# Sparse attention and a feed-forward layer on one core: the local heads in blocks of 32 queries, turned by VectorE and small transfers

## The chip, the core and the metric

The kernel runs on one core of a Trainium2 chip. The core has TensorE (PE, matrix products), VectorE (DVE), ScalarE (ACT), GpSimd (POOL) and SyncE (SP, which here issues all transfers). The metric is the device time of one execution in microseconds (us). Three runs of the kernel before took 927.29, 929.12 and 929.34 us, a median of 929.12.

## The reference

Attention over 8 batches, 8 heads, 576 tokens and 64 channels a head, followed by a feed-forward layer over the 4608 tokens. Four heads see the last 32 tokens ("local"), four see every 32nd token ("strided").

```python
scores = scale * np.matmul(q, k.transpose(0, 1, 3, 2))
rel = pos[:, None] - pos[None, :]
mask_local = (rel >= 0) & (rel < stride)                       # stride = 32
mask_strided = (rel >= 0) & (pos[None, :] % stride == pos[:, None] % stride)
masks = [mask_local if h < H // 2 else mask_strided for h in range(H)]
attn = softmax(np.where(masks, scores, -1e9))
x = np.matmul(attn, v)                                         # to (4608, 512)
h = x @ w_in                                                   # (512, 2048)
return (0.5 * h * (1.0 + erf(h / sqrt(2)))) @ w_out            # (2048, 512)
```

## The kernel before

**The feed-forward layer** sets the frame. The tokens are cut into 12 tiles of 384. For each tile 16 steps run, one for each block of 128 hidden channels, so there are 192 steps, numbered n = 0 to 191. In a step `ffn_h(n)` (L537 to L539) multiplies the tile's x by a block of w_in into a bank H of PSUM: twelve products of 384 columns, since x and w are each split into a high and a low part. `ffn_g(n)` takes the GELU on ACT (L546), rounds it on ACT (gh, L548), and forms the rest gl on DVE (L550). `ffn_o(n)` (L576 to L578) adds nine products of 512 columns to three banks O. H has two banks, so step n + 2 can begin its H only when gl of step n has read the bank. `ffn_o(n)` is issued two steps after `ffn_h(n)`.

**The strided heads** are done by DVE alone: a long row of small products and sums (L412, L454), which are given out over the steps by their estimated cost, in advance of the tile that needs them.

**The local heads** are cut into 36 jobs of 128 tokens (two windows of 64 queries, each with 96 keys, four heads); three jobs fill one tile. `local_job(x)` makes, in this order: scores of 64 queries against 96 keys on PE, into the four column blocks of one bank (L247); masking with a running minimum on DVE (L204); the exponential on ACT (L209); the sum's reciprocal on DVE (L213, L216); the scaling by it on ACT (L225); four transpositions on PE (L253); the copy of their result out of PSUM on ACT (L255); the products with v on PE (L262); and the split of the result into the high and low part of x, xh on ACT (L229) and xl on DVE (L231). Jobs 0 to 5 belong to the opening, whose order is written out by hand in a table. The 30 jobs from 6 on belong to the main loop, which begins at step 16: `stage(n)` moves every job under way on by two parts a step, and `starts` says at which step a job begins, every fifth step as a rule. So PE meets a job in three places: scores, transpositions three steps later, and products with v one step after these.

**What sets the order.** In the main loop only ACT follows the order in which the code is written. A scheduler places the instructions of PE, DVE, POOL and SP, by its own estimate of when their inputs are ready; every engine then executes its own list in order, and waits where an input is missing. SP's list holds the loads of q and k (`qk`), of v (`vl`), of the strided heads' data (`sq`, `sk`, `sv`), and the stores of the result (`ob`). POOL builds the masks and clears the strided scores (`sc`, L405).

Of the kernel before, what the change touches and what calls it, by code (L numbers as in the profile page):

```python
# [10 lines left out]
F32 = mybir.dt.float32  # L11
# [20 lines left out]
NEG = -8.0e9  # L32
# [13 lines left out]
NB = 16  # L46
# [33 lines left out]
LPLACE = [(b, r // 2) for _, b, r in ROWS[::2]]  # L80
# [3 lines left out]
def attn_ffn_kernel(ctx: ExitStack, tc: tile.TileContext, qk, vl, qka, va, qs, ks, vs, w, out):  # L84
    nc = tc.nc
    NJ = qk.shape[0]
    NR, D = qs.shape[2:]
    S = NR * STRIDE
    HL = P // STRIDE
    NT, DM = out.shape  # L90
    NF = w.shape[0]
    NC = DM // P
    NU = len(PLACE)
    NV = len(VISITS)
    NTILE = NT // TT
# [12 lines left out]
    lpool = ctx.enter_context(tc.tile_pool(name="lpool", bufs=2))  # L108
# [3 lines left out]
    ps_a = ctx.enter_context(tc.tile_pool(name="ps_a", bufs=1, space=bass.MemoryType.PSUM))  # L112
# [2 lines left out]
    smask = const.tile([P, MA], F32, name="smask")  # L115
    mask = const.tile([P, LK], F32, name="mask")
    mask0 = const.tile([P, LK], F32, name="mask0")

    def rows(j):
        return slice(j * D, (j + 1) * D)  # L120
# [4 lines left out]
    def slot(name, shape, dtype=F32):  # L125

        return wpool.tile(shape, dtype, name=name, tag="w")
# [41 lines left out]
    def x_tile(t):  # L169
        if t not in xt:  # L170
            xt[t] = [xpool.tile([P, NC, TT], F32R, name=f"x{i}_{t}", tag=f"x{i}{t % 2}") for i in "hl"]
        return xt[t]


    jq, jv = {}, {}
    loaded = set()

    def load_jq(x):
        if x < NJ and ("q", x) not in loaded:
            loaded.add(("q", x))  # L180
            jq[x] = lpool.tile([P, 2 * N2 * (LU + LK)], F32, name=f"qk_{x}", tag="qk", bufs=3)
            nc.sync.dma_start(jq[x], qk[x])

    def load_jv(x):
        if x < NJ and ("v", x) not in loaded:
            loaded.add(("v", x))
            jv[x] = lpool.tile([LK, 2, HL, D], F32, name=f"vl_{x}", tag="vl", bufs=4)
            nc.sync.dma_start(jv[x], vl[x])

    def buffers(name, pn):  # L190
        n = 4 * LK
        if pn >= 0:
            return pbig[pn][:, 0:n], pbig[pn][:, n:n + DM]
        return (lpool.tile([P, n], F32, name=f"P_{name}", tag="P", bufs=2),
                lpool.tile([P, DM], F32, name=f"PT_{name}", tag="PT", bufs=2))

    def small(name):
        return [lpool.tile([P, 4], F32, name=f"{k}_{name}", tag=k, bufs=4) for k in ("nm", "ss", "rs")]
# [29 lines left out]
    def to_x(dh_, dl_, src):  # L228
        nc.scalar.copy(dh_, src)  # L229
        yield  # L230
        nc.vector.tensor_tensor(dl_, src, dh_.bitcast(F32), ALU.subtract)  # L231

    def local_job(x, banks=None, dve=0, pn=-1):

        s, pt = [pl.tile([P, DM], F32, name=f"S{i}_L{x}", tag=tg)
                 for i, (pl, tg) in enumerate(banks or ((ps_a, "S0"), (ps_a, "S1")))]
        p, pts = buffers(f"L{x}", pn)
        nb = 2 * N2
        blocks = [slice(i * LK, (i + 1) * LK) for i in range(nb)]
        qv = jq[x][:, 0:nb * LU].rearrange("p (i t) -> p i t", t=LU)  # L240
        kv = jq.pop(x)[:, nb * LU:].rearrange("p (i t) -> p i t", t=LK)
        msk = [mask0 if LPLACE[2 * x + i % 2][1] == 0 else mask for i in range(nb)]
        steps = softmax_parts(blocks, P, lambda i: s[:, blocks[i]], lambda i: msk[i], p,
                              *small(f"L{x}"), dve)
        for i, cs in enumerate(blocks):
            for j in (i % 2, 1 - i % 2):
                nc.tensor.matmul(s[rows(j), cs], qv[rows(j), i, :], kv[rows(j), i, :], start=True, stop=True)  # L247
        for st in steps:
            yield
            st()  # L250
        yield
        for i, cs in enumerate(blocks):
            nc.tensor.transpose(pt[:LK, i * P:(i + 1) * P], p[:, cs], ident)  # L253
        yield
        nc.scalar.copy(pts[:LK, 0:nb * P], pt[:LK, 0:nb * P])  # L255
        yield
        xp = s if banks else ps_a.tile([P, DM], F32, name=f"X_L{x}", tag="X")
        xv = xp[:, 0:N2 * P].rearrange("p (a q) -> p a q", a=N2)
        for i in range(nb):
            pr, a = divmod(i, 2)  # L260
            for j in range(2):
                nc.tensor.matmul(xv[rows(j), pr, a * LU:(a + 1) * LU], jv[x][:, a, 2 * pr + j, :],  # L262
                                 pts[:LK, i * P + j * LU:i * P + (j + 1) * LU], start=True, stop=True)
        jv.pop(x)
        if x >= JPT:
            load_jv(x + 3)
        yield
        t, c0 = divmod(x * P, TT)
        dst = [a[:, 0:N2, c0:c0 + P] for a in x_tile(t)]
        yield from to_x(*dst, xv)  # L270


# [91 lines left out]
    for vi in range(NA, NV):  # L364
        n = VISITS[vi][2]
# [163 lines left out]
    ready = [t * NF for t in range(NTILE)]  # L529
    xfree = [0, 0] + ready[1:-1]  # L530

    def ffn_h(n):
        t, f = divmod(n, NF)
        xh, xl = xt[t]
        hp = ps_h.tile([P, TT], F32, name=f"H_{n}", tag="H")
        for c in range(NC):
            nc.tensor.matmul(hp, w1[f][:, 0, c, :], xh[:, c, :], start=(c == 0), stop=False)  # L537
            nc.tensor.matmul(hp, w1[f][:, 0, c, :], xl[:, c, :], start=False, stop=False)  # L538
            nc.tensor.matmul(hp, w1[f][:, 1, c, :], xh[:, c, :], start=False, stop=(c == NC - 1))  # L539
        hps[n] = hp  # L540
# [78 lines left out]
    for j in range(2):  # L619
        nc.gpsimd.affine_select(mask[rows(j)], mask[rows(j)], pattern=[[-1, LK]], compare_op=ALU.is_ge,  # L620
                                fill=NEG, base=STRIDE, channel_multiplier=1)
        nc.gpsimd.affine_select(mask[rows(j)], mask[rows(j)], pattern=[[1, LK]], compare_op=ALU.is_ge,
                                fill=NEG, base=-1, channel_multiplier=-1)
    nc.gpsimd.tensor_copy(mask0[:, STRIDE:], mask[:, STRIDE:])
    nc.gpsimd.memset(mask0[:, 0:STRIDE], NEG)
    for h in range(HL):
        m = smask[h * 32:(h + 1) * 32]
        nc.gpsimd.iota(m.bitcast(I32), pattern=[[-1, MA]], base=0, channel_multiplier=1)
# [54 lines left out]
    for nm in "qkv":  # L683
        load_strided(order_g[1], nm)

    active = []

    def start_local(x, **kw):
        active.append([local_job(x, **kw), x, 0])
        advance(active[-1])  # L690
        load_jq(x + 3)

    def advance(e, k=2):
        for _ in range(k):
            if next(e[0], True) is not None:
                active.remove(e)
                break
        e[2] += 1

    def stage(n):  # L700
        if any(e[2] == 1 for e in active):
            flush_exps(NU)
        for e in list(active):
            if e[2] < 4 or n >= xfree[e[1] // JPT]:
                advance(e)

    starts = {}
    for i in range(JPT):
        for t in range(2, NTILE):
            starts[max(NB, ready[t - 1] + 5 * i - 2)] = t * JPT + i  # L710

    def step(n):
        c = n // NF
        while splits and n >= xfree[splits[0][0]]:
            for _ in splits.pop(0)[1]():
                pass
        if c > 0:
            stage(n)
        if n in starts:
            start_local(starts[n])  # L720
        if c + 1 < NTILE:
            a, e = ready[c] + (1 if c == 0 else 0), ready[c + 1]
            need = last[c] + (last[c + 1] - last[c]) * min(1.0, max(0.0, (n - a + 1) / (e - a - 2)))
            run_strided(max(need, tot * (n - N0) / (ready[-1] - 2 - N0)))
        if NB <= n < NS:
            ffn_h(n)
            for _ in ffn_g(n):
                pass
        if n == NS + 1:
            ffn_o(n - 3, n - 2)  # L730
        elif n >= NB + 2 and n < NS:
            ffn_o(n - 2)
        if n >= NB + 2 and (n - 2) % NF == NF - 1:
            store((n - 2) // NF)

    with tc.manual_schedule(engines={ET.Activation}):
        for n in range(NB, NS + 1):
            step(n)
    with tc.manual_schedule(engines={ET.Activation, ET.PE}):
# [66 lines left out]
```

## Time and profile before

| | |
|---|---|
| runs | 927.29, 929.12, 929.34 us |
| profiled execution, whole | 928.01 us |
| its span from first to last instruction | 926.2 us |
| mean granted clock of TensorE | 0.987 |
| DMA, mean | 67 GB/s, share of the 16 engines 20% |

The span covers the opening up to about 115 us, in which weights are loaded and split and x for the first tiles is made; then the main loop to about 922 us; then one last copy and store. In the timelines each row gives the start in us, the length in us, the engine, the line of the code, the operation, what it writes and reads with shapes, and in brackets the idle time before it with what ended it. Matrix products overlap in their lengths, so their pace is read from one start to the next. PEld is the load of a product's stationary operand. On DVE too, short instructions overlap and are read from start to start.

### The profile page before, as it was taken

The numbers are of one execution on the slowest core, as the hardware profiler recorded it, in microseconds if no ns is written. First come the engines' busy times: TensorE is split into PE (matmuls) and PEld (weight loads), VectorE is DVE, ScalarE is ACT, GpSimd is POOL, SyncE is SP. The second block draws the span as 40 slices with busy tenths as digits, with TensorE's granted clock in tenths as the row PEclk, the third lists the DMA queues.
The fourth block names the chain that finished last, engine by engine and source line by source line (L and its number), as shares of the span: only waits on it lengthen the run. The fifth ranks groups of instructions, "written<-read, shape, count | busy, mean of one in ns | idle before, by whom it ended". The sixth has DMA issues, their size and how long they took to land.

```text
span 926.2 us, 17928 instructions
## 1 busy us (share of the span) xinstructions
PE 897.7 (97%) x5588; PEld 791.2 (85%) x5588; DVE 703.7 (76%) x4834; ACT 490.6 (53%) x1115; POOL 8.0 (1%) x56
## 2 busy tenths in 40 slices
PE   4499999999999999999999999999999999999998
PEld 4388888888888888888888888888888888889997
DVE  6899998578994999669959967968999897661110
ACT  6899675356555554446445435436455445542322
POOL 1000000000000000000000000000000000000000
PEclk9699999999999999999999999999999999999999
DMA  9991122011030112002201121011202100100001
GB/s 316 355 347 66 50 73 75 24 58 49 10 109 24 50 38 86 25 24 83 69 24 58 50 69 58 24 50 58 69 10 83 58 16 22 39 1 1 35 1 35
DMA packets 21872, 62.24 MB, mean 67 GB/s; under 512 B 2576, under 2 KB 3856, under 8 KB 19728
## 3 DMA queue, kind: packets, MB, share of 16 engines
q1 hardware_dynamic: 21776, 61.09, 19.7%
q8 instruction: 44, 0.72, 0.3%
q14 instruction: 52, 0.43, 0.1%
HBM read 51.64 MB, written 9.44 MB: 66 GB/s over the span
## 4 chain that ended last, share of the span: by engine, by line
PE 94%; DMA 3%; ACT 2%; SPq 0%; issue 0%
PE H L537 15%; PE H L539 15%; PE O L578 14%; PE O L577 14%; PE H L538 14%; PE O L576 14%; PE S_L L247 3%; DMA ws<-in_w_dram 2%; PE X_L L262 2%; PE S_L L253 2%; DMA qk<-in_qk_dram 1%; ACT w L158 1%; ACT ws L144 0%; ACT L546 0%; ACT ws L150 0%; PE S_L L262 0%
## 5 line engine op out<-in xcount | busy, mean ns | idle before, releaser
L537 PE MATMUL H<-xh,w 128*128 128x384 f32 x768 | 265.7, 346 | 5.7 <-DVE gl L550 3.0
L539 PE MATMUL H<-xh,w 128*128 128x384 f32 x768 | 261.9, 341 | 0.0
L538 PE MATMUL H<-xl,w 128*128 128x384 f32 x768 | 259.3, 338 | 0.0
L546 ACT ACTIVATE H<-H 128x384 f32<-128x384 f32 x192 | 91.2, 475 | 301.8 <-PE H L539 273.9
L454 DVE SCALAR_TENSOR_TENSOR acc<-sv,sc,acc 128x64 f32<-128x64 f32 x1158 | 244.2, 276 | 0.6
L577 PE MATMUL O<-w,gh 128*128 128x512 f32 x576 | 227.4, 395 | 0.0
L578 PE MATMUL O<-w,gl 128*128 128x512 f32 x576 | 226.8, 396 | 0.0
L576 PE MATMUL O<-w,gh 128*128 128x512 f32 x576 | 225.0, 391 | 0.0
L550 DVE TENSOR_TENSOR gl<-H,gh 128x384 fp32r<-128x384 f32 x192 | 105.9, 552 | 138.3 <-ACT gh L548 137.6
L412 DVE CUSTOM_DVE_ANT_0 junk<-sq,sk 128x64 f32<-128x64 f32 x1290 | 204.1, 217 | 0.0
L537 PEld LDWEIGHTS H<-xh,w 128*128 128x128 f32 x768 | 145.3, 189 | 15.8 <-DVE gl L550 3.6
L538 PEld LDWEIGHTS H<-xl,w 128*128 128x128 f32 x768 | 145.3, 189 | 5.7 <-DVE xl L231 0.2
L539 PEld LDWEIGHTS H<-xh,w 128*128 128x128 f32 x768 | 145.1, 189 | 1.7
L578 PEld LDWEIGHTS O<-w,gl 128*128 128x128 f32 x576 | 107.9, 187 | 22.7
L576 PEld LDWEIGHTS O<-w,gh 128*128 128x128 f32 x576 | 108.4, 188 | 18.0
L577 PEld LDWEIGHTS O<-w,gh 128*128 128x128 f32 x576 | 108.0, 188 | 18.3
L412 DVE DVE_READ_ACCUMULATOR2_ANT sc<- 128x1 f32 x1290 | 103.9, 81 | 0.0
L548 ACT CAST gh<-H 128x384 fp32r<-128x384 f32 x192 | 92.2, 480 | 6.0
L546 ACT ACT_TABLE_LOAD x39 | 50.0, 1283 | 0.7
L209 ACT ACTIVATE P_L<-P_L,nm_L 128x96 f32<-128x96 f32 x136 | 48.9, 362 | 0.0
L422 ACT ACT_TABLE_LOAD x35 | 44.9, 1283 | 0.6
L255 ACT COPY PT_L<-S_L 96x512 f32<-96x512 f32 x34 | 19.8, 582 | 46.3 <-PE S_L L253 46.3
(86 smaller groups left out, 587.0 us busy)
## 6 DMA issues: line engine op xcount, KB each, us to landing
ws<-in_w_dram SPq DMA_DIRECT2D x16, 1024.0 KB, 15.4
qk<-in_qk_dram SPq DMA_DIRECT2D x36, 320.0 KB, 3.0
out_dram<-ob SPq DMA_DIRECT2D x34, 256.0 KB, 2.2
vl<-in_vl_dram SPq DMA_DIRECT2D x36, 192.0 KB, 2.7
sk<-in_ks_dram SPq DMA_DIRECT2D x8, 576.0 KB, 4.9
sv<-in_vs_dram SPq DMA_DIRECT2D x8, 576.0 KB, 3.7
sq<-in_qs_dram SPq DMA_DIRECT2D x4, 576.0 KB, 3.7
sq<-in_qs_dram SPq DMA_DIRECT2D x3, 448.0 KB, 3.2
```

Source lines behind the costliest of these rows:

```text
L209: nc.scalar.activation(p[:nq, cs], p[:nq, cs], AF.Exp, bias=nmax[:nq, i:i + 1], scale=-1.0, accum_out=ssum[:nq, i:i + 1])
L412: nc.vector.tensor_tensor_reduce(junk, sq[vi, "q"][:, r0 + r, :], sq[vi, "k"][:, c, :], 1.0, 0.0, ALU.mult, ALU.add, ss[u][:, r, c:c + 1])
L454: nc.vector.scalar_tensor_tensor(acc[:, r, :], sq[vi, "v"][:, c, :], wgt, acc[:, r, :], ALU.mult, ALU.add)
L537: nc.tensor.matmul(hp, w1[f][:, 0, c, :], xh[:, c, :], start=(c == 0), stop=False)
L538: nc.tensor.matmul(hp, w1[f][:, 0, c, :], xl[:, c, :], start=False, stop=False)
L539: nc.tensor.matmul(hp, w1[f][:, 1, c, :], xh[:, c, :], start=False, stop=(c == NC - 1))
L546: nc.scalar.activation(hp, hp, AF.Gelu)
L548: nc.scalar.copy(gh, hp)
L550: nc.vector.tensor_tensor(gl, hp, gh.bitcast(F32), ALU.subtract)
L576: nc.tensor.matmul(o, gh[:, sl], w2[f][:, 0, :], start=(f == 0), stop=False)
L577: nc.tensor.matmul(o, gh[:, sl], w2[f][:, 1, :], start=False, stop=False)
L578: nc.tensor.matmul(o, gl[:, sl], w2[f][:, 0, :], start=False, stop=(f == NF - 1))
```

## The change

For jobs 6 to 35 `band_job` takes the place of `local_job`.

- **Scores** are computed by blocks of 32 queries against the 64 keys that these can see, so 16 products of 64 rows by 32 columns of PE with 64 columns each, in place of 8 of 64 by 64 with 96. The eight positions of that size on PE are used in turn, with two banks, one for each half of the rows.
- **The mask** has 64 columns in place of 96, in three versions (`bmask`), built on POOL in the opening.
- **Softmax**: the minimum is taken on DVE and the exponential on ACT as before, on 64 columns a head. The scaling by the reciprocal moves from ACT to DVE, one instruction for the four heads.
- **Transposition**: DVE transposes 32 by 32 squares within the same partitions (one instruction of 256 columns), and eight transfers of 32 partitions by 512 bytes put the squares in place in a buffer `band`, which POOL has cleared once. It has room for three jobs. The four transpositions on PE and the copy out of PSUM on ACT are gone.
- **Products with v** read `band`; their number and size stay.
- **The order**: a job has one place on PE, the pulse. At the pulse of job x stand the products with v of job x - 1 and then the scores of job x, ahead of that step's H. The exponential follows one step later, the rest of the softmax and the transfers two steps later. The pulses are at steps 16, 20, 24, then at 28, 34, 39 and so on by 6, 5, 5 steps, up to a last one at 172. PE now follows the written order in the main loop, as ACT does; DVE, POOL and SP are placed by the scheduler as before.

```diff
+    bmask = {i: const.tile([P, 2 * STRIDE], F32, name=f"bmask{i}") for i in (None, 0, 1)}
...
+    def band_job(x, bt):
+        QB = STRIDE
+        s = [ps_a.tile([P, DM], F32, name=f"S{j}_L{x}", tag=f"S{j}") for j in range(2)]
...
+        for h in range(0, HL, 2):
+            for g in range(P // QB):
+                a, b = divmod(g, 2)
+                for j in range(2):
+                    nc.tensor.matmul(s[j][g * QB:(g + 1) * QB, head[h][1]],
+                                     qv[rows(j), h // 2, a, b * QB:(b + 1) * QB],
+                                     kv[rows(j), h // 2, a, b * QB:(b + 2) * QB],
+                                     start=True, stop=True, tile_position=(j * D, g * QB))
+        yield
...
+        for h in range(HL):
+            j, cs = head[h]
+            nc.vector.tensor_tensor_reduce(p1[:, h * 2 * QB:(h + 1) * 2 * QB], s[j][:, cs], msk, -SC, 3.0e38,
+                                           ALU.add, ALU.min, nm[:, h:h + 1])
+        yield
+        for h in range(HL):
+            nc.scalar.activation(pv[:, :, h, :], p1[:, h * 2 * QB:(h + 1) * 2 * QB].rearrange(
+                "p (c t) -> p c t", c=2), AF.Exp, bias=nm[:, h:h + 1], scale=-1.0, accum_out=ss[:, h:h + 1])
+        yield
+        nc.vector.tensor_scalar_add(ss, ss, 1e-9)
+        nc.vector.reciprocal(rs, ss)
+        nc.vector.tensor_tensor(pv, pv, rs.unsqueeze(1).unsqueeze(3).to_broadcast([P, 2, HL, QB]), ALU.mult)
+        nc.vector.transpose(pt, pb)
+        tv = pt.rearrange("p (c q) -> p c q", c=2)
+        for g in range(P // QB):
+            for c in range(2):
+                kb = g % 2 + c
+                nc.sync.dma_start(bt[kb * QB:(kb + 1) * QB, g, :], tv[g * QB:(g + 1) * QB, c, :])
+        yield
...
+                    nc.tensor.matmul(xv[rows(j), r, a * LU:(a + 1) * LU], jv[x][:, a, 2 * r + j, :],
+                                     bv[:LK, a, :, 2 * r + j, :], start=True, stop=True)
...
+    for i, m in bmask.items():
+        nc.gpsimd.memset(m, 0.0)
+        for g in range(P // STRIDE):
+            sl = slice(g * STRIDE, (g + 1) * STRIDE)
+            nc.gpsimd.affine_select(m[sl], m[sl], pattern=[[-1, 2 * STRIDE]], compare_op=ALU.is_ge,
+                                    fill=NEG, base=STRIDE, channel_multiplier=1)
...
-    starts = {}
-    for i in range(JPT):
-        for t in range(2, NTILE):
-            starts[max(NB, ready[t - 1] + 5 * i - 2)] = t * JPT + i
+    PULSES = [NB, NB + 4, NB + 8] + [ready[t - 1] + o for t in range(3, NTILE) for o in (-4, 2, 7)]
+    PULSES.append(ready[NTILE - 1] - 4)
...
+    band = slot("band", [P, 4 * DM])
+    nc.gpsimd.memset(band, 0.0)
...
+    def before(n):
+        for d, p in ((1, 2), (2, 3)):
+            if n - d in pulse_at:
+                if d == 1:
+                    flush_exps(NU)
+                part(J0 + pulse_at[n - d], p)
+    def pulse(n):
+        if n in pulse_at:
+            x = J0 + pulse_at[n]
+            part(x - 1, 4)
+            part(x, 0)
+            part(x - 1, 5, 6)
+            part(x, 1)
...
-        if c > 0:
-            stage(n)
-        if n in starts:
-            start_local(starts[n])
+        before(n)
+        pulse(n)
...
-    with tc.manual_schedule(engines={ET.Activation}):
+    with tc.manual_schedule(engines={ET.Activation, ET.PE}):
         for n in range(NB, NS + 1):
             step(n)
```

Three places show what moved. The first is PE's list around job 10, whose scores are S0_L10, whose transposed weights are S1_L10 and whose product with v is X_L10. Before, it stands in three places:

```order
L578 MATMUL O_2_2_2583<-w_0_398,gl_32_2464 128x512
L247 MATMUL S0_L10_2594<-qk_10_1584 64x96 x8
L537 MATMUL H_35_2630<-xh_2_1651,w_3_528 128x384
...
L578 MATMUL O_2_2_2583<-w_3_528,gl_35_2644 128x512
L253 MATMUL S1_L10_2595<-ident_85,P_L10_2596 96x128 x4
L537 MATMUL H_38_2792<-xh_2_1651,w_6_774 128x384
...
L538 MATMUL H_39_2844<-xl_2_1652,w_7_728 128x384
L262 MATMUL X_L10_2819<-PT_L10_2597,vl_10_1853 64x64 x8
L539 MATMUL H_39_2844<-xh_2_1651,w_7_728 128x384
```

In the changed kernel the product X_L10 stands with the scores of job 11 (S0_L11 and S1_L11, 16 products in turn) in one place ahead of step 39, and there are no transpositions:

```order
L639 MATMUL O_2_2_2729<-w_4_698,gl_36_2833 128x512
L324 MATMUL X_L10_2944<-band_1443,vl_10_2005 64x64 x8
L287 MATMUL S0_L11_2955<-qk_11_2319 32x64
L287 MATMUL S1_L11_2956<-qk_11_2319 32x64
...
L598 MATMUL H_39_2999<-xh_2_1719,w_7_808 128x384
```

So three interruptions of the H and O products became one, and an interruption now holds the work of two jobs.

The second place is DVE's list from job 10's sum (ss_L10) on; the strided heads' sums (acc_10) stand between. First the kernel before, then the changed one:

```order
L213 TENSOR_SCALAR ss_L10_2599<-ss_L10_2599 128x4
L452 TENSOR_SCALAR acc_10_2737<-sv_4_1361,sc_10_2248 128x64 x2
L216 RECIPROCAL rs_L10_2600<-ss_L10_2599 128x4
L454 SCALAR_TENSOR_TENSOR acc_10_2737<-sv_4_1361,sc_10_2248,acc_10_2737 128x64 x11
L550 TENSOR_TENSOR gl_36_2698<-H_36_2684,gh_36_2697 128x384
```

```order
L308 TENSOR_SCALAR ss_L10_2688<-ss_L10_2688 128x4
L513 TENSOR_SCALAR acc_10_2867<-sv_4_1441,sc_10_2389 128x64 x2
L309 RECIPROCAL rs_L10_2689<-ss_L10_2688 128x4
L515 SCALAR_TENSOR_TENSOR acc_10_2867<-sv_4_1441,sc_10_2389,acc_10_2867 128x64 x2
L310 TENSOR_TENSOR PT_L10_2686<-PT_L10_2686,rs_L10_2689 128x256
L515 SCALAR_TENSOR_TENSOR acc_10_2867<-sv_4_1441,sc_10_2389,acc_10_2867 128x64 x2
L311 STREAM_TRANSPOSE PT_L10_2686<-PT_L10_2686 128x256
L515 SCALAR_TENSOR_TENSOR acc_10_2867<-sv_4_1441,sc_10_2389,acc_10_2867 128x64 x3
L611 TENSOR_TENSOR gl_35_2773<-H_35_2759,gh_35_2772 128x384
```

Two instructions came in on DVE, the scaling and the transposition, and both stand ahead of the gl of the step after the pulse (step 34).

The third place is SP's list at the same job; qk_13 and vl_13 are loads for job 13, sv_5 one for the strided heads, ob_1 the stores of tile 1. First before, then changed:

```order
L585 DMA out_0_dram<-ob_1_2_2531 128x512
L188 DMA vl_13_2828<-in_vl_dram 96x512
L182 DMA qk_13_2613<-in_qk_dram 128x640
L389 DMA sv_5_2895<-in_vs_dram 128x1152
L188 DMA vl_14_3165<-in_vl_dram 96x512
```

```order
L190 DMA vl_13_2953<-in_vl_dram 96x512
L646 DMA out_0_dram<-ob_1_2_2647 128x512
L184 DMA qk_13_2975<-in_qk_dram 128x640
L316 DMA band_1443<-PT_L10_2686 32x128 x8
L450 DMA sv_5_3033<-in_vs_dram 128x1152
L190 DMA vl_14_3299<-in_vl_dram 96x512
```

The eight transfers of a job came in between loads that were next to each other.

More of the change, by code (lines that the diff above doesn't have):

```diff
@@ L269, in local_job @@
         dst = [a[:, 0:N2, c0:c0 + P] for a in x_tile(t)]
+        yield from to_x(*dst, xv)
+    def band_job(x, bt):
+        QB = STRIDE
+        s = [ps_a.tile([P, DM], F32, name=f"S{j}_L{x}", tag=f"S{j}") for j in range(2)]
+        qv = jq[x][:, 0:2 * N2 * LU].rearrange("p (r a t) -> p r a t", r=N2, a=2)
+        kv = jq.pop(x)[:, 2 * N2 * LU:].rearrange("p (r a t) -> p r a t", r=N2, a=2)
+        head = [(h % 2, slice(h // 2 * 2 * QB, (h // 2 + 1) * 2 * QB)) for h in range(HL)]
+        for h in range(0, HL, 2):
[7 more added lines that the diff above has]
+        yield
+        p1 = lpool.tile([P, 4 * LK], F32, name=f"P_L{x}", tag="P", bufs=2)
+        p2 = lpool.tile([P, DM], F32, name=f"PT_L{x}", tag="PT", bufs=2)
+        pb, pt = p2[:, 0:DM // 2], p2[:, DM // 2:]
+        pv = pb.rearrange("p (c h t) -> p c h t", c=2, h=HL)
+        nm, ss, rs = small(f"L{x}")
+        first_ = [a for a in range(2) if LPLACE[2 * x + a][1] == 0]
+        msk = bmask[first_[0] if first_ else None]
+        for h in range(HL):
[17 more added lines that the diff above has]
+        yield
+        xp = ps_a.tile([P, DM], F32, name=f"X_L{x}", tag="X")
+        xv = xp[:, 0:N2 * P].rearrange("p (r q) -> p r q", r=N2)
+        bv = bt.rearrange("p (a b) (h q) -> p a b h q", a=2, h=HL)
+        for r in range(N2):
+            for a in range(2):
+                for j in range(2):
+                    nc.tensor.matmul(xv[rows(j), r, a * LU:(a + 1) * LU], jv[x][:, a, 2 * r + j, :],
+                                     bv[:LK, a, :, 2 * r + j, :], start=True, stop=True)
+        jv.pop(x)
+        load_jv(x + 3)
+        yield
+        t, c0 = divmod(x * P, TT)
+        dst = [d[:, 0:N2, c0:c0 + P] for d in x_tile(t)]
@@ L625, in attn_ffn_kernel @@
     nc.gpsimd.memset(mask0[:, 0:STRIDE], NEG)
+    for i, m in bmask.items():
[4 more added lines that the diff above has]
+                                    fill=NEG, base=STRIDE, channel_multiplier=1)
+            nc.gpsimd.affine_select(m[sl], m[sl], pattern=[[1, 2 * STRIDE]], compare_op=ALU.is_ge,
+                                    fill=NEG, base=-1, channel_multiplier=-1)
+            if i is not None and g == 2 * i:
+                nc.gpsimd.memset(m[sl, 0:STRIDE], NEG)
     for h in range(HL):
@@ L684, in attn_ffn_kernel, with part @@
         load_strided(order_g[1], nm)
[L686 to L705, printed above, removed]
-    starts = {}
-    for i in range(JPT):
-        for t in range(2, NTILE):
-            starts[max(NB, ready[t - 1] + 5 * i - 2)] = t * JPT + i
+    J0 = 2 * JPT
+    PULSES = [NB, NB + 4, NB + 8] + [ready[t - 1] + o for t in range(3, NTILE) for o in (-4, 2, 7)]
+    PULSES.append(ready[NTILE - 1] - 4)
+    pulse_at = {n: k for k, n in enumerate(PULSES)}
+    local = {}
+    band = slot("band", [P, 4 * DM])
+    nc.gpsimd.memset(band, 0.0)
+    NBT = 3
+    bts = [band[:, i * DM:(i + 1) * DM].rearrange("p (g q) -> p g q", g=4) for i in range(NBT)]
+    def part(x, *which):
+        for p in which:
+            if J0 <= x < NJ:
+                if p == 0:
+                    local[x] = [band_job(x, bts[x % NBT]), 0]
+                assert local[x][1] == p
+                local[x][1] += 1
+                if next(local[x][0], True) is not None:
+                    load_jq(x + 3)
+    def before(n):
[11 more added lines that the diff above has]
+            part(x, 1)
     def step(n):
```

## The prediction

> **What bounds the kernel now.** First the page: who is busy, and what the chain that ended last is made of.
>
> ```profile
> span 926.2 us, 17928 instructions
> PE 897.7 (97%) x5588; PEld 791.2 (85%) x5588; DVE 703.7 (76%) x4834; ACT 490.6 (53%) x1115; POOL 8.0 (1%) x56
> PE 94%; DMA 3%; ACT 2%; SPq 0%; issue 0%
> ```
>
> The chain is PE, nearly from end to end. Then the busy times by stretch (us, then busy us of PE, PEld, DVE, ACT, POOL, granted clock, DMA share, GB/s), for the main loop and for its two fullest stretches on DVE.
>
> ```profile
> 115.00:925.00 810.00, 807.36 (x4785) 712.71 (x4783) 604.28 (x4506) 398.33 (x946) 4.17 (x31) 1.00 0.14 44
> 200.00:280.00 80.00, 80.00 (x489) 70.45 (x488) 72.41 (x582) 43.49 (x99) 0.66 (x5) 1.00 0.19 62
> 680.00:760.00 80.00, 80.00 (x477) 70.42 (x476) 74.67 (x575) 38.88 (x95) 0.43 (x3) 1.00 0.15 48
> ```
>
> PE is busy for 807 of 810 us at a granted clock of 1.00. So in the main loop a microsecond that PE no longer needs is one that the kernel no longer takes, as long as PE's inputs come in time. The second stretch has 7.6 us left on DVE, the third 5.3.
>
> **What a job costs PE now.** The timeline shows job 10's three places between H (L537, L538) and O (L576 to L578).
>
> ```profile
> 202.28 0.39 PE L576 MATMUL O<-w,gh 128*128 128x512 f32 x1
> 202.51 0.40 PE L577 MATMUL O<-w,gh 128*128 128x512 f32 x1
> 202.75 0.40 PE L578 MATMUL O<-w,gl 128*128 128x512 f32 x1
> 203.07 0.88 PE L247 MATMUL S_L<-qk 64*64 64x96 f32 x16
> 203.88 0.44 PE L537 MATMUL H<-xh,w 128*128 128x384 f32 x1
> 204.16 0.34 PE L538 MATMUL H<-xl,w 128*128 128x384 f32 x1
> 204.33 0.34 PE L539 MATMUL H<-xh,w 128*128 128x384 f32 x1
> ...
> 216.29 0.39 PE L578 MATMUL O<-w,gl 128*128 128x512 f32 x1
> 216.52 0.60 PE L253 MATMUL S_L<-ident,P_L 128*96 128x128 f32 x4
> 216.88 0.43 PE L537 MATMUL H<-xh,w 128*128 128x384 f32 x1
> 217.14 0.33 PE L538 MATMUL H<-xl,w 128*128 128x384 f32 x1
> ...
> 221.30 0.34 PE L538 MATMUL H<-xl,w 128*128 128x384 f32 x1
> 221.57 0.69 PE L262 MATMUL X_L<-PT_L,vl 96*64 96x64 f32 x16
> 222.18 0.44 PE L539 MATMUL H<-xh,w 128*128 128x384 f32 x1
> 222.47 0.34 PE L537 MATMUL H<-xh,w 128*128 128x384 f32 x1
> ```
>
> From start to start an O product takes 0.23 us (202.28 to 202.51) and an H product 0.17 (204.16 to 204.33). What a place costs is the time from when the next ordinary product was due to when the pace is back. Scores: due at 202.75 + 0.23 = 202.98, pace back at 204.16 - 0.17 = 203.99, so 1.01 us. Transpositions: 216.52 to 216.97, 0.45. Products with v: 221.47 to 222.30, 0.83. Together **2.29 us a job**. The scores begin 0.09 us after they were due, the products with v 0.10; the first H behind either takes 0.11 more than its pace.
>
> **What a job costs PE after.** The products with v keep their number and shapes: 0.10 to enter, 0.61 (221.57 to 222.18), and 0.12 to leave, with the scores now between these and H. Going from one tile shape to the other I charge as entering the scores today, 0.09. The new scores are the unknown: 16 products in eight positions, 32 records. The trace has the same positions' size (64 by 32) once, in the opening, with the old scores beside it at the same slower clock.
>
> ```profile
> 9.36 1.92 PE L305 MATMUL A<-qka 64*32 64x24 f32 x128 [2.87 <-DMA qka<-in_qka_dram]
> 11.21 1.09 PE L253 MATMUL S_L<-ident,pbig 128*96 128x128 f32 x4
> 16.82 1.55 PE L247 MATMUL S_L<-qk 64*64 64x96 f32 x16
> 18.30 1.05 PE L253 MATMUL S_L<-ident,pbig 128*96 128x128 f32 x4
> ```
>
> 128 records took 1.85 us there, 14.5 ns each; the old scores took 1.48 us there and 0.81 in the main loop, a factor of 1.83. So 32 records come to 0.46 us at that pace, 0.25 at the main loop's. These products had 24 columns, the new ones 64. By columns: the old scores go two side by side, four pairs of 96 columns in 0.81 us, 2.1 ns a column; eight side by side make two rounds of 64, 0.27 us. Bounds: 0.25 if only the records count; 1.08 if they still go by twos (8 x 64 x 2.1 ns); 1.62 if each record costs what one costs today (0.81 / 16 = 51 ns). I take **0.30**, near the row of the same shape.
>
> One place of a job then costs 0.10 + 0.61 + 0.09 + 0.30 + 0.12 = 1.22 us, **1.07 less**. Thirty jobs make **32.1 us**.
>
> [...]
>
> **What it adds elsewhere, and what hides it.** DVE, with the nearest rows:
>
> ```profile
> 204.19 0.25 DVE L204 CUSTOM_DVE_ANT_0 P_L<-S_L,mask 128x96 f32<-128x96 f32 x1
> 204.37 0.25 DVE L204 CUSTOM_DVE_ANT_0 P_L<-S_L,mask 128x96 f32<-128x96 f32 x1
> 520.98 0.22 DVE L412 CUSTOM_DVE_ANT_0 junk<-sq,sk 128x64 f32<-128x64 f32 x1
> 521.13 0.22 DVE L412 CUSTOM_DVE_ANT_0 junk<-sq,sk 128x64 f32<-128x64 f32 x1
> L462 DVE STREAM_TRANSPOSE xs<-acc 128x256 f32<-128x256 f32 (+1 forms) x37 | 15.2, 412 | 0.8
> L231 DVE TENSOR_TENSOR xl<-X_L,xh 128x256 fp32r<-128x256 f32 x30 | 12.5, 418 | 5.9 <-ACT xh L229 5.9
> ```
>
> Four masked minima go from 0.18 to about 0.15 us each (the same operation on 64 columns at 520.98), -0.12; the scaling of 256 columns costs about 0.42 (as L231) and the transposition 0.41 (as L462). Net +0.71 us a job, 21 us in all. DVE had 810 - 604 = 206 us free in the main loop and keeps 206 - 21 - 32 = 153. In the fullest stretch, with some 3.5 jobs, 3.5 x (0.71 + 1.07) = 6.2 us goes from 5.3 that are left: there the cover is gone and about 1 us is lost, unless the next stretch takes it up. ACT loses its scalings and the copy:
>
> ```profile
> 212.73 1.18 ACT L225 ACTIVATE P_L<-P_L,rs_L 128x96 f32<-128x96 f32 x4
> 217.16 0.58 ACT L255 COPY PT_L<-S_L 96x512 f32<-96x512 f32 x1 [1.53 <-PE S_L L253]
> ```
>
> That is 1.76 us a job less on an engine half idle: worth nothing by itself, but gh comes no later.
>
> **The new path to X_L** must fit between two pulses.
>
> ```profile
> 210.26 0.17 DVE L213 TENSOR_SCALAR ss_L<-ss_L 128x4 f32<-128x4 f32 x1 [0.61 <-ACT P_L L209]
> 210.67 0.17 DVE L216 RECIPROCAL rs_L<-ss_L 128x4 f32<-128x4 f32 x1
> 197.62 1.52 SPq L585 DMA_DIRECT2D out_dram<-ob  x3
> DMA to landing us min/median/max: 2.0/2.2/4.3
> ```
>
> In job 10 the exponentials end and the sum begins at 210.26, 7.2 us after the scores began. The reciprocal, scaling and transposition, with strided sums between, bring it to about 212.4. Eight issues at 1.52 / 3 = 0.51 us take SP 4.1, and the last lands 2.2 later (the stores' median): 218.7, some **15.6 us after the scores**. A step of H and O is 12 x 0.174 + 9 x 0.23 = 4.2 us, so three gaps of 4 steps give 18 us with a place of 1.2, eighteen of 5 give 22, nine of 6 give 26. It fits with 2.4 us or more to spare and costs nothing; past that, each microsecond is a wait of PE at the head of its list, with scores, H and O queued behind. SP had nothing else to do for most of that time; loads behind the eight wait 4.1 us more, and those are asked for a job or more ahead.
>
> **PE in written order.** It now waits in place for gl, where the scheduler chose before.
>
> ```profile
> 212.89 0.55 DVE L550 TENSOR_TENSOR gl<-H,gh 128x384 fp32r<-128x384 f32 x1
> ```
>
> This gl belongs to step 36, the one held up by the exponentials; it ends at 213.44, and H of step 38, which needs its bank, starts at 216.88: 3.4 us to spare in the worst step of a job. Only at step 20 does DVE's new list look longer: 54 strided products stand between gl of steps 19 and 20 (21 before), 54 x 0.15 = 7.9 us, with four minima, two xl and gl itself 9.6 us, against 4.2 + 1.2 of PE. That is 4.2 us over, 3.4 of which are spare. I take **1 us** there, bounds 0 and 4.
>
> **The opening.** POOL builds three more masks, 29 instructions of about 0.26 us, 7 us, in part ahead of DVE's first input. The chain has this there:
>
> ```profile
> 15.27 19.00 DMA ws<-in_w_dram
> ```
>
> All of PE's H work waits for those weights to 34.3 us, so the delay is hidden; without that cover it would be up to 7 us. Clearing `band` once on POOL is off the path.
>
> **Sum**, against the profiled execution (928.0 us; its span of 926.2 and 1.8 around it): 928.0 - 32.1 + 1 = **897 us**. The profiled execution lies 1.1 under the median of the runs, within their spread of 2.1.
>
> **The rivals.**
> 1. *The positions take turns.* If the scores go by twos, a place costs 2.00 and the sum is 928 - 8.7 + 1 = 920. If every record costs today's 51 ns, it costs 2.54, 0.25 more than now, and the kernel is **slower, 936**. The point that decides is 1.37 us for the scores. For it: records of 64 by 64 show no better today. Against it: the row of 64 by 32. Chances 11% and 5%. [...]
> 2. *`band` comes late.* If the eight transfers are served one after the other at 2.2 us each, they take 17.6 in place of 6.3, and X_L is ready 27 us after the scores: 3 x 9 + 18 x 5 + 9 x 1 = 126 us of waits, over 1000 us. It turns slower than now from about 23 us. Against it: three stores issued together landed in 2.2. 4%.
> 3. *DVE becomes the bound in places.* If each of the ten stretches of 80 us were short by 1 us as the fullest is, or the pulses cost PE half a microsecond each for gl: 10 to 15 us given back, 910. For it: 93% in one stretch. Against: the mean is 75%. 14%.
>
> **How the numbers follow.** The forecast has 66%, with 890 to 906 of its own (scores at 0.25 and no change of shape between: 36 us gained, 892; DVE's waits at step 20 at 4 us and scores at 0.5: 906). With rival 3 and most of the first half of rival 1, 890 to 918 holds 8 in 10. A measurement here tells 0.2%, about 2 us, from no change. Faster: 66 + 14 + 11 = 91, of which 3 go to a mixture of rivals that ends within that; slower: 5 + 4 = 9. So 0.88, 0.03 and 0.09.
>
> **What would show it.** Right: no L253 of these jobs on PE, one place a job of about 1.2 us with scores of 0.3, PE still busy all through the main loop, no idle time before X_L. Wrong: scores over 0.5 us from first to last start; idle time of PE before X_L ended by a DMA (rival 2); or before H ended by gl (rival 3).

## The result, and the profile after

The changed kernel takes **903.55 us** (median of four runs, 902.33 to 904.64), the kernel before beside it 928.20 (four runs, 926.96 to 929.34): a ratio of 0.9734, interval 0.9714 to 0.9754, so 24.65 us or 2.7% less. The forecast of 897 lies 6.5 us below, the range of 890 to 918 holds it. The profiled execution took 902.33 us, 25.7 less than that of before.

The first lines of the changed kernel's page: the span, the busy times with their shares, and the chain that ended last.

```profile
span 900.6 us, 19161 instructions
...
PE 869.3 (97%) x5948; PEld 772.4 (86%) x5948; DVE 716.2 (80%) x4894; ACT 443.5 (49%) x969; POOL 16.4 (2%) x86
...
PE 92%; ACT 3%; DMA 3%; SPq 1%; issue 0%; DVE 0%
```

PE is still the chain and has 28.4 us less to do. Its windows in the main loop (us, then busy us of PE, PEld, DVE, ACT, POOL, granted clock, DMA share, GB/s):

```profile
120.00:200.00 80.00, 75.32 (x501) 66.70 (x501) 67.48 (x496) 36.19 (x88) 0.50 (x4) 0.96 0.15 45
200.00:840.00 640.00, 640.00 (x4313) 571.57 (x4310) 536.69 (x3979) 298.08 (x680) 3.67 (x27) 1.00 0.17 54
```

From 200 us on PE never rests, at a clock of 1.00. But between 120 and 200 it is idle for 4.7 us, and its clock is 0.96: something goes wrong early. First a place as it was meant to be, in PE's timeline at job 10's products with v and job 11's scores:

```profile
221.33 0.40 PE L639 MATMUL O<-w,gl 128*128 128x512 f32 x1
221.66 0.69 PE L324 MATMUL X_L<-band,vl 96*64 96x64 f32 x16
222.28 0.45 PE L287 MATMUL S_L<-qk 64*32 64x64 f32 x32
222.66 0.44 PE L598 MATMUL H<-xh,w 128*128 128x384 f32 x1
222.94 0.34 PE L599 MATMUL H<-xl,w 128*128 128x384 f32 x1
```

Due at 221.33 + 0.23 = 221.56, pace back at 222.94 - 0.17 = 222.77: 1.21 us, against 2.29 in three places before. Thirty jobs save 30 x 1.08 = 32.4 us. Now the place of step 20, where job 6's products with v stand (the bracket is the idle time before a row and what ended it):

```profile
129.92 0.40 PE L639 MATMUL O<-w,gl 128*128 128x512 f32 x1
132.37 0.34 PE L324 MATMUL X_L<-band,vl 96*64 96x64 f32 x4 [2.05 <-DMA band<-PT_L]
134.76 0.91 PE L324 MATMUL X_L<-band,vl 96*64 96x64 f32 x12 [2.05 <-DMA band<-PT_L]
135.60 0.68 PE L287 MATMUL S_L<-qk 64*32 64x64 f32 x32
136.21 0.69 PE L598 MATMUL H<-xh,w 128*128 128x384 f32 x1
136.69 0.52 PE L599 MATMUL H<-xl,w 128*128 128x384 f32 x1
137.01 0.52 PE L600 MATMUL H<-xh,w 128*128 128x384 f32 x1
```

PE waits for `band` twice, 2.05 us each, 4.1 us in all, with four records of X_L between. These are all such waits of the kernel: PE's list of waits has one line for X_L.

```profile
PE X_L L324 <- DMA band<-PT_L: 4.1, 2, 2.1
```

Behind the wait an H product takes 0.32 us (136.69 to 137.01) in place of 0.17. The windows around it, PE alone (busy us, clock, DMA share, GB/s), say why:

```profile
130.00:135.00 5.00, 0.89 (x11) 0.92 0.11 24
135.00:141.00 6.00, 6.00 (x58) 0.50 0.32 91
141.00:147.00 6.00, 6.00 (x30) 1.00 0.00 0
```

The clock granted after the two waits is 0.50 for about 6 us. In these the last twelve records with v take 0.84 us (134.76 to 135.60) in place of 12/16 of 0.62, the scores 0.61 in place of 0.38, the H of the step 4.0 (136.21 to 140.21) in place of 2.1, the first O products some 0.4 more: about 2.9 us beside the 4.1. By this account 928.0 - 32.4 + 4.1 + 2.9 + 0.6 (a wait for gl, below) = 903.2, against 902.3 measured.

Why was `band` late? The last piece of job 6's scores on PE with the first H and the first O behind it, and that job's rows on DVE and SP (with a gl that stands between):

```profile
116.42 0.31 PE L287 MATMUL S_L<-qk 64*32 64x64 f32 x6
116.66 0.44 PE L598 MATMUL H<-xh,w 128*128 128x384 f32 x1
...
122.94 0.17 DVE L308 TENSOR_SCALAR ss_L<-ss_L 128x4 f32<-128x4 f32 x1 [0.36 <-ACT PT_L L305]
...
123.03 0.39 PE L637 MATMUL O<-w,gh 128*128 128x512 f32 x1
...
125.24 0.56 DVE L611 TENSOR_TENSOR gl<-H,gh 128x384 fp32r<-128x384 f32 x1 [0.99 <-ACT gh L609]
...
125.94 0.42 DVE L310 TENSOR_TENSOR PT_L<-PT_L,rs_L 128x256 f32<-128x256 f32 x1
...
127.51 0.44 DVE L311 STREAM_TRANSPOSE PT_L<-PT_L 128x256 f32<-128x256 f32 x1
...
128.03 5.37 SPq L316 DMA_DIRECT2D band<-PT_L  x8
```

The product was due at 129.92 + 0.23 = 130.15, only 13.7 us after 116.42: the scores of job 6 stand in four pieces between the opening's last O products, the last piece just ahead of H. Behind them PE makes the H of three steps, from 116.66 to 123.03, with no O between, because a step's O is issued two steps after its H and the main loop's first O is that of step 16, issued at step 18. So the gap holds the H of four steps but the O of two only, and 2 x 9 x 0.23 = 4.1 us are missing in it against a gap later on. On DVE the scaling queued behind a gl that itself waited 0.99 us for gh, and the eight issues took 5.4 us. The last transfer was there at 134.7, 18.3 us after the last piece of the scores began.

A job in the steady part, for comparison: its scores, its transfers' issue, and its product with v five steps later.

```profile
341.22 0.45 PE L287 MATMUL S_L<-qk 64*32 64x64 f32 x32
...
351.41 4.95 SPq L316 DMA_DIRECT2D band<-PT_L  x8
...
362.39 0.40 PE L639 MATMUL O<-w,gl 128*128 128x512 f32 x1
362.71 0.69 PE L324 MATMUL X_L<-band,vl 96*64 96x64 f32 x16
```

The last of the eight issues starts at 355.8 and ends at 356.4. The DMA issues of the page put the landing 1.8 us behind the start of an issue (the median of 240):

```profile
band<-PT_L SPq DMA_DIRECT2D x240, 16.0 KB, 1.8
```

So `band` is there at 357.6, 16.4 us after the scores and 5.0 before it is due (362.39 + 0.23). Read alike from the issues and landings of the trace, the paths of jobs 7 to 35 take 14.7 to 19.0 us.

### The profile page after: what moved, and what is told of

The parts are those of the page before. It is cut to its first block, busy times and chain, and to the rows that moved or that the text cites. A ratio compares the mean times of both kernels' runs of the same rounds, so it can differ in the third digit from the quotient of the medians.

```text
span 900.6 us, 19161 instructions
## 1 busy us (share of the span) xinstructions
PE 869.3 (97%) x5948; PEld 772.4 (86%) x5948; DVE 716.2 (80%) x4894; ACT 443.5 (49%) x969; POOL 16.4 (2%) x86
## 4 chain that ended last, share of the span: by engine, by line
PE 92%; ACT 3%; DMA 3%; SPq 1%; issue 0%; DVE 0%
PE H L598 15%; PE O L639 15%; PE O L638 15%; PE H L600 15%; PE H L599 14%; PE O L637 14%; PE X_L L324 2%; DMA ws<-in_w_dram 2%; PE S_L L287 1%; DMA vl<-in_vl_dram 1%; ACT w L160 1%; ACT ws L152 1%; ACT ws L146 0%; SPq L316 0%; ACT L607 0%
## 5 line engine op out<-in xcount | busy, mean ns | idle before, releaser
L515 DVE SCALAR_TENSOR_TENSOR acc<-sv,sc,acc 128x64 f32<-128x64 f32 x1158 | 248.3, 276 | 0.7
L638 PEld LDWEIGHTS O<-w,gh 128*128 128x128 f32 x576 | 108.4, 188 | 18.3
L473 DVE DVE_READ_ACCUMULATOR2_ANT sc<- 128x1 f32 x1290 | 106.4, 82 | 0.0
L305 ACT ACTIVATE PT_L<-P_L,nm_L 128x64 f32<-128x64 f32 x120 | 39.9, 333 | 0.0
L231 ACT CAST xh<-X_L 128x256 fp32r<-128x256 f32 x30 | 11.2, 372 | 38.9 <-PE X_L L324 38.7
```

Source lines behind the costliest of these rows:

```text
L473: nc.vector.tensor_tensor_reduce(junk, sq[vi, "q"][:, r0 + r, :], sq[vi, "k"][:, c, :], 1.0, 0.0, ALU.mult, ALU.add, ss[u][:, r, c:c + 1])
L515: nc.vector.scalar_tensor_tensor(acc[:, r, :], sq[vi, "v"][:, c, :], wgt, acc[:, r, :], ALU.mult, ALU.add)
L638: nc.tensor.matmul(o, gh[:, sl], w2[f][:, 1, :], start=False, stop=False)
```

## The experiments

The theory: the saving on PE is as forecast, the 6.5 us that are missing come from the one late `band` at step 20, its wait and the slow clock behind it. Rivals: PE in written order costs something all along; the positions do take turns; DVE or the transfers give something back in many places. Each kernel was timed beside the kernel before on the same chip; "base" is the first experiment's kernel. The experiments ran on three chips. The kernel before took 928.20 us beside the change, 926.61 beside experiments 1, 4, 6 and the first kernel of 3, 926.80 beside experiments 2, 5, 8 and 9, and 927.85 beside experiment 7 and the second kernel of 3. A difference of medians between two of these groups is uncertain by these 1 to 2 us.

**1. Later first pulses (the base).** The first three gaps become 5, 4 and 4 steps, the fourth 5 in place of 6.

```diff
-    PULSES = [NB, NB + 4, NB + 8] + [ready[t - 1] + o for t in range(3, NTILE) for o in (-4, 2, 7)]
+    PULSES = [NB, NB + 5, NB + 9] + [ready[t - 1] + o for t in range(3, NTILE) for o in (-4 + (t == 3), 2, 7)]
```

> The changed kernel with the first pulses at steps 16, 21, 25, 29, 34 in place of 16, 20, 24, 28, 34, so that the first products with v have one step more for their transfers. Theory (the 6.5 us that are missing to the forecast come from one late X_L6: 4.1 us of waiting for band and some 2.5 us of lower granted clock behind it): no idle time of PE before X_L, granted clock 1.00 from 120 to 200 us, 896.5 us, within 1.5. Rival (the missing time is spread over many small waits for gl, or the places cost more than 1.22 us): over 901.

Measured: 897.10 us (896.94 to 897.58), ratio 0.9689 (0.9674 to 0.9703). The same window as above, and from PE's timeline the one wait for `band` that is left, at the second pulse:

```profile
120.00:200.00 80.00, 78.49 (x560) 69.40 (x560) 67.83 (x512) 42.06 (x94) 0.50 (x4) 1.00 0.21 64
```

```profile
154.29 0.57 PE L324 MATMUL X_L<-band,vl 96*64 96x64 f32 x12 [0.90 <-DMA band<-PT_L]
```

The clock stays at 1.00. With one step more for the first transfer path the kernel takes 6.45 us less than the change by the medians, 5.1 by the profiled executions and 4.9 by what each saves against the kernel before beside it (29.5 and 24.65). The forecast's 897 is reached with nothing else touched; the saving of 29.5 is 1.5 short of the forecast's 31.

**2. Gaps of 5, 5, 4.**

```diff
-    PULSES = [NB, NB + 5, NB + 9] + [ready[t - 1] + o for t in range(3, NTILE) for o in (-4 + (t == 3), 2, 7)]
+    PULSES = [NB, NB + 5, NB + 10] + [ready[t - 1] + o for t in range(3, NTILE) for o in (-4 + 2 * (t == 3), 2 + (t == 3), 7)]
```

> The changed kernel with the first pulses at steps 16, 21, 26, 30, 35, 39. Theory (e1_later_pulses still waits 0.9 us before one X_L and loses nothing else there): no wait before X_L, 896.2 us, 0.9 less than e1_later_pulses. Rival (a later third job delays x of tile 2): more than e1_later_pulses by a wait of H at step 32.

Measured: 896.21 us (895.65 to 897.12), ratio 0.9678 (0.9646 to 0.9710). No wait for `band` is left. It has the lowest median of all versions here, though the 0.9 us to the base, taken on another chip, are too little to tell.

**3. PE by the scheduler**, with the change's own pulses.

```diff
-    with tc.manual_schedule(engines={ET.Activation, ET.PE}):
+    with tc.manual_schedule(engines={ET.Activation}):
```

> The changed kernel with the order of PE in the main loop left to the scheduler, as in the kernel before. Theory (the written order costs only the wait at step 20, since an H could have gone ahead of the late X_L6): 897 to 900 us, no idle time before X_L6. Rival (the written order gains by itself, the scheduler's scatters the scores among O and H): over 905, with scores interrupted.

Measured: 898.05 us (897.98 to 898.27), ratio 0.9699 (0.9684 to 0.9713). PE is busy for 80.00 of the 80 us from 120 on: free to put other products ahead of X_L, it has no wait at step 20. So written order is not slow by itself; it only makes a late input stop everything behind it. The same edit on experiment 2's pulses:

> The first pulses of e8_five_five_four with the order of PE in the main loop left to the scheduler as in e4_scheduler_pe. Theory (each takes away the same wait, so together they gain no more than one): within 1.5 us of e8_five_five_four. Rival (the scheduler's order gains by itself): 2 us or more less.

896.73 us (894.41 to 899.50), ratio 0.9667 (0.9637 to 0.9696), no different from experiment 2. Once no input is late, it does not matter who orders PE.

**4. Two places a job** (base with the products with v one step behind the scores).

```diff
-            part(x - 1, 4)
             part(x, 0)
-            part(x - 1, 5, 6)
             part(x, 1)
+        if n - 1 in pulse_at:
+            part(J0 + pulse_at[n - 1] - 1, 4, 5, 6)
```

> As e1_later_pulses, but the products with v of job x - 1 stand one step behind the scores of job x, so that a job has two places on PE again. Theory (a place costs about 0.09 to enter and 0.12 to leave, and the change of tile shape inside a common place 0.09): 0.1 to 0.2 us more a job, 3 to 6 us more than e1_later_pulses. Rival (one place has no worth of its own): same as e1_later_pulses within 1 us.

Measured: 902.27 us (899.28 to 904.36), ratio 0.9741 (0.9712 to 0.9770), 5.2 above the base. The two places in its PE timeline:

```profile
409.40 0.40 PE L639 MATMUL O<-w,gl 128*128 128x512 f32 x1
409.72 0.45 PE L287 MATMUL S_L<-qk 64*32 64x64 f32 x32
410.11 0.44 PE L598 MATMUL H<-xh,w 128*128 128x384 f32 x1
410.39 0.34 PE L599 MATMUL H<-xl,w 128*128 128x384 f32 x1
...
414.15 0.40 PE L639 MATMUL O<-w,gl 128*128 128x512 f32 x1
414.48 0.69 PE L324 MATMUL X_L<-band,vl 96*64 96x64 f32 x16
415.09 0.44 PE L598 MATMUL H<-xh,w 128*128 128x384 f32 x1
415.37 0.33 PE L599 MATMUL H<-xl,w 128*128 128x384 f32 x1
```

Scores: 409.63 to 410.22, 0.59; products with v: 414.38 to 415.20, 0.82; together 1.41, 0.20 more than in one place, 6 us in thirty jobs. The scores take 0.39 from first to next (409.72 to 410.11) whether they stand alone here or behind X_L (222.28 to 222.66, 0.38). So nothing visible is paid for the change from one tile shape to the other; what one place saves is one entering (0.09) and one leaving (0.11).

**5. The old scores** (base with the eight products of 64 by 64 by 96; the columns are then read wrongly, so the local heads' result is another).

```diff
-        for h in range(0, HL, 2):
-            for g in range(P // QB):
...
-                for j in range(2):
-                    nc.tensor.matmul(s[j][g * QB:(g + 1) * QB, head[h][1]],
...
+        for i in range(2 * N2):
+            for j in (i % 2, 1 - i % 2):
+                nc.tensor.matmul(s[i // 2][rows(j), i % 2 * LK:(i % 2 + 1) * LK], qv[rows(j), i // 2, i % 2],
+                                 kv[rows(j), i // 2, i % 2], start=True, stop=True)
```

> As e1_later_pulses, but the scores are made in the old form, 8 products of 64 by 64 with 96 columns, put into the two banks as they fall, so that the softmax then works on other columns than it should and the local heads' result is not the reference's; all else is done as before. Theory (the form of the scores is worth what its row says): scores take 0.81 us in place of 0.30 behind the change of shape, a place 1.73 in place of 1.21, 30 x 0.52 = 16 us more than e1_later_pulses, 913. Rival (the old scores were dear because they stood alone between O and H): less than 6 us more.

Measured: 910.62 us (907.85 to 912.47), ratio 0.9828 (0.9796 to 0.9860), 13.5 above the base. Its place in PE's timeline:

```profile
412.21 0.69 PE L320 MATMUL X_L<-band,vl 96*64 96x64 f32 x16
412.82 0.88 PE L285 MATMUL S_L<-qk 64*64 64x96 f32 x16
413.63 0.45 PE L594 MATMUL H<-xh,w 128*128 128x384 f32 x1
```

0.81 us (412.82 to 413.63) against 0.39: 0.42 a job, 12.7 in thirty. Almost half of the base's gain is the form of the scores.

**6. Same position twice in a row** (base, another order of the loops, so that two consecutive products share a position).

```diff
-        for h in range(0, HL, 2):
-            for g in range(P // QB):
-                a, b = divmod(g, 2)
-                for j in range(2):
+        for g in range(P // QB):
+            a, b = divmod(g, 2)
+            for j in range(2):
+                for h in range(0, HL, 2):
```

> As e1_later_pulses, but the 16 score products are issued so that two that follow each other have the same position on PE. Theory (scores are cheap because products in different positions run side by side): the second of each pair waits for the first, scores go from about 0.4 to about 1.0 us a job, 30 x 0.6 = 18 us more than e1_later_pulses, about 915. Rival (the cost is set by the number and size of the records, whatever their positions): same time as e1_later_pulses within 2 us.

Measured: 900.03 us (898.64 to 902.50), ratio 0.9724 (0.9700 to 0.9747), 2.9 above the base. In the trace the scores take 0.44 us from first to next (408.12 to 408.56), 0.05 more, 1.5 us in all. The large cost that side by side work seemed to demand (18 us by the estimate above) didn't come, so this run could not tell whether the positions take turns. Two more do.

**7. Sixteen further products** behind the scores, into columns that nobody reads; in the first kernel in the eight positions in turn, in the second all in two.

```diff
+        for i in range(8):
+            g = i % 4
+            for j in range(2):
+                nc.tensor.matmul(s[j][g * QB:(g + 1) * QB, 128 + i // 4 * 64 + 0:][:, 0:64],
+                                 qv[rows(j), i // 4, g // 2, g % 2 * QB:(g % 2 + 1) * QB],
+                                 kv[rows(j), i // 4, g // 2, g % 2 * QB:(g % 2 + 2) * QB],
+                                 start=True, stop=True, tile_position=(j * D, g * QB))
```

And the second against the first:

```diff
-                nc.tensor.matmul(s[j][g * QB:(g + 1) * QB, 128 + i // 4 * 64 + 0:][:, 0:64],
+                nc.tensor.matmul(s[j][0 * QB:(0 + 1) * QB, 128 + i // 4 * 64 + i % 4 * 64:][:, 0:64],
...
-                                 start=True, stop=True, tile_position=(j * D, g * QB))
+                                 start=True, stop=True, tile_position=(j * D, 0 * QB))
```

> As e1_later_pulses, but behind the 16 score products of a job stand 16 more of the same size, in the same eight positions, into columns that nobody reads. Both theories: what 16 products cost in eight positions, about 0.25 to 0.3 us a job by the record pace, 8 to 9 us more than e1_later_pulses, 905 to 906.

> As e12_more_eight, but the 16 further products all go to two of the eight positions, eight after one another in each, into columns that nobody reads. Theory (products run side by side in different positions and one after another in the same): by the old scores' pace of 2.1 ns a column by twos, 1.08 us a job, 32 us more than e1_later_pulses, 929. Rival (the number of records sets the cost, whatever their positions): the same as e12_more_eight within 2 us.

Measured: 908.96 us (908.45 to 909.85), ratio 0.9800 (0.9774 to 0.9826), for eight positions; 923.38 (921.62 to 925.23), ratio 0.9958 (0.9933 to 0.9983), for two. Against the base 11.9 and 26.3 us, 0.40 and 0.88 a job (0.35 and 0.83 by the savings against the kernel before). The two differ by 14.4 us, where the rival allowed 2; the theory's 929 for two positions was 5.6 too high, and eight positions cost 3 us more than expected. A place of each in PE's timeline, eight positions first (the real scores are L287, the further ones L294):

```profile
410.92 0.46 PE L287 MATMUL S_L<-qk 64*32 64x64 f32 x32
411.19 0.59 PE L294 MATMUL S_L<-qk 64*32 64x64 f32 x32
411.71 0.45 PE L605 MATMUL H<-xh,w 128*128 128x384 f32 x1
```

```profile
416.56 0.46 PE L287 MATMUL S_L<-qk 64*32 64x64 f32 x32
416.83 1.14 PE L294 MATMUL S_L<-qk 64*32 64x64 f32 x32
417.90 0.44 PE L605 MATMUL H<-xh,w 128*128 128x384 f32 x1
```

From the first score to H it is 0.79 us and 1.34, so the same sixteen products cost 0.40 more than the base's 0.39 in eight positions and 0.95 more in two. By the trace a product cost 25 ns in eight positions and 59 in two, so the positions did not take turns here; at the place of job 11 in the changed kernel, eight score records start within the 0.05 us from 222.28. Still, four times the positions brought a factor of 2.2 (by the medians) to 2.4, not 4.

**8. Every transfer twice** (base).

```diff
-        for g in range(P // QB):
+        for g in [g for g in range(P // QB) for _ in range(2)]:
```

> As e1_later_pulses, but each of the eight transfers of a job is issued twice. Theory (the path to X_L is hidden with several us to spare in gaps of 5 and 6 steps and hardly in those of 4): X_L is ready some 5 us later, PE waits only at the first three or four pulses, 5 to 15 us more than e1_later_pulses in all, none after 200 us. Rival (transfers cost at every pulse, by their issue on SP or by contention with loads): 25 us or more, spread over the whole loop.

Measured: 942.85 us (937.64 to 944.25), ratio 1.0168 (1.0129 to 1.0208), 45.8 above the base and slower than the kernel before. The theory of 5 to 15 us with no wait after 200 us was wrong, and what its rival named came: over 25 us, with waits over the whole loop. Its list of waits, then from the timelines of SP and of PE a job's issues and its product with v:

```profile
PE X_L L324 <- DMA band<-PT_L: 23.7, 12, 4.9
```

```profile
367.68 9.94 SPq L316 DMA_DIRECT2D band<-PT_L  x15
378.34 0.51 SPq L316 DMA_DIRECT2D band<-PT_L  x1
```

```profile
381.64 0.57 PE L324 MATMUL X_L<-band,vl 96*64 96x64 f32 x12 [2.34 <-DMA band<-PT_L]
```

Sixteen issues take 11 us in place of 5, which is 6 us more than the path had, and the spare in a gap of five steps was 5.0. The median landing is 1.8 us as before, so it is mainly SP's issuing, one after the other, that makes the path long; the last transfer of the job shown landed only 3.3 us after its issue, with loads of `sq` and `sk` issued beside it. PE waits at the same products for another 5.4 us for which the list names no releaser. From 120 to 200 us, where the gaps are shortest, the granted clock falls to 0.89.

**9. The transposition on DVE twice** (base).

```diff
         nc.vector.transpose(pt, pb)
+        nc.vector.transpose(pt, pb)
```

> As e1_later_pulses, but VectorE makes each transposition of squares twice, 0.37 to 0.41 us more a job, 11 to 12 us more of DVE in all. Theory (DVE has room, the work added to it is hidden): within 1.5 us of e1_later_pulses. Rival (DVE sets the pace in its full stretches): 5 to 12 us more, with idle time of PE before H ended by gl after 200 us.

Measured: 902.23 us (900.54 to 902.66), ratio 0.9737 (0.9709 to 0.9764), 5.1 above the base, where the theory allowed 1.5. Its window of the main part, and from PE's timeline the longest of the waits that pay for it:

```profile
200.00:840.00 640.00, 640.00 (x4310) 571.60 (x4307) 546.20 (x4025) 298.17 (x680) 3.69 (x27) 1.00 0.18 54
```

```profile
136.78 0.57 PE L325 MATMUL X_L<-band,vl 96*64 96x64 f32 x12 [1.62 <-DMA band<-PT_L]
```

From 200 us on PE has no idle time though DVE does 9.5 us more than in the window of the change: DVE's work as such is hidden. The loss lies in the first pulses, where `band` is late by 4.3 us in four waits, with the granted clock at 0.72 from 135 to 141 us. There the path had nothing to spare, as the base's wait of 0.9 had shown, and it grew by more than the 0.4 us of an instruction: at job 6 the second transposition stands 1.5 us behind the first on DVE (127.90 and 129.39), and the issues begin at 129.92, in the base at 128.48.

## Why the prediction was right, and where it was not

**What bounds the kernel**: right. PE is busy throughout from 200 us on (640.00 of 640 us), and what PE no longer does (28.4 us), the kernel no longer takes, but for some 3 us (25.7 by the profiled executions).

**A job on PE**: right, 1.21 us against 1.22. Inside it two terms were off, and that they cancel was luck: the scores take 0.38 to 0.39, not 0.30, and the change of tile shape nothing visible, not 0.09 (the scores take 0.38 behind X_L and 0.39 alone, experiment 4). The row behind the 0.30 was scaled by its slower clock. The granted clock on record does not show that (1.00 from 9.36 to 11.21 us, 0.50 from 16.82 to 18.30); the scaling rests on the transpositions next to it, 1.09 and 1.05 us long against 0.60 in the main loop. That the positions do not take turns is shown by experiment 7 (25 ns a product in eight positions, 55 to 59 in two), which refutes rival 1.

**DVE, ACT and the opening**: right. Scaling and transposition on DVE take their 0.42 and 0.44 us and stay hidden from 200 us on (in experiment 9 PE is busy for 640.00 of 640 us with the transposition made twice), so rival 3 is refuted. DVE's busy time rose by 12.5 us (703.7 to 716.2 on the two pages); the 21 us of the sum count the new instructions at full length, though these overlap their neighbours (the transposition from 127.51 is 0.44 long, the next gl starts at 127.87). DVE's first use of the masks waits until 5.70 us, by the list of waits for POOL; in the kernel before it began at 5.39, behind the scores. H of step 16 begins at 116.7 us in both kernels, so that is hidden too. The 54 products between gl of steps 19 and 20 make 8.1 us at 0.15, not 7.9, and the 1 us charged there for gl did not come; at H of step 19 stands a wait of 0.58 us for gl that the kernel before did not have:

```profile
125.85 0.45 PE L598 MATMUL H<-xh,w 128*128 128x384 f32 x1 [0.58 <-DVE gl L611]
```

**The step that failed** is the path to X_L: "It fits with 2.4 us or more to spare and costs nothing". Both sides of it were off at the first pulse. The path was reckoned at 15.6 us: 7.2 to the sum, 2.1 from there to the first issue, 4.1 for the issues, 2.2 for the last landing. The steady job above has 6.7, 3.5, 4.95 and 1.2, in all 16.4; job 6 has 6.5, 5.1, 5.4 and 1.3, in all 18.3. So the large miss is the 2.1 us, since scaling and transposition wait their turn on DVE behind strided sums and gl; an issue of these transfers takes 0.62 us (4.95 / 8) and not the stores' 0.51. The gap was reckoned at 18 us from steady steps; at the border of opening and main loop, where two steps have no O yet, it was 13.7. A full gap of four steps is tight as well: in the base the second product resumes 18.6 us after the scores (135.72 to 154.29), having waited 0.9. The prediction did name what follows, a wait of PE at the head of its list, but not that the clock granted behind the two waits here would be 0.50 for about 6 us, which made 4.1 us into about 7. Experiments 1 and 3 show it: with one step more, or with PE free to go on, 897 and 898 come out. Of the prediction's signs of being wrong this one appeared, idle time before X_L ended by a DMA, in one place. That 903.55 still lies inside the forecast's own 890 to 906 is in part luck, because that room was laid for gl at step 20 and slower scores. Rival 2 had the right place and the wrong mechanism: the transfers are not served one after the other, but they are issued so (eight issues in 4.95 us, the last landing 1.2 behind them), and experiment 8 shows that twice that would have made the change slower than the kernel before.

**Where the 24.65 us come from**, by steps against the base, which saves 29.5: the form of the scores 13.5 (experiment 5), one place in place of two 5.2 (experiment 4), and by rows 30 x 0.45 = 13.5 for the transpositions, which no run put back alone. That is 32.2, and the 2.7 us above 29.5 stay open. The late `band` takes back 4.9 of the 29.5 (experiment 1).

## What to carry to other kernels

Work that moves off the bound engine becomes latency, and its slack is to be checked at the shortest gap, which was here the first one behind the opening (13.7 us, where the path took 18.3), and not in a steady iteration; one row of a table of steps was worth 5 to 6.5 us. Of the eight small transfers from one queue the issuing counted here (8 x 0.62 us), more than the landing (1.8 us). On an engine in written order, put a late input's user as late as the order allows, since everything behind it waits (4.1 us here), and on PE count the pause's aftermath too (about 2.9 us here).

## What the runs showed of the hardware

- After two waits of 2.05 us with four records between, PE's granted clock was 0.50 for about 6 us (135 to 141 us), about 2.9 us of loss. The length of a wait alone did not tell when: behind a wait of 1.62 us (experiment 9) an H product took 0.32 us, behind one of 2.34 (experiment 8, at 381 us) it took its usual 0.17. What lowers the clock no run here shows.
- Sixteen products of 64 by 32 with 64 columns took 0.39 us in eight positions, 25 ns each, and 0.88 to 0.95 in two, 55 to 59 ns each (experiment 7).
- Going from products of 128 by 128 to smaller ones and back cost 0.09 to 0.11 us each way, going from those of 96 by 64 to those of 64 by 32 nothing that can be seen (the scores took 0.38 us behind them and 0.39 alone, experiment 4).
